# Filter phases by matmul with the turn's fraction left in PSUM, factors kept on chip, spatial weights transposed straight to their use

## The chip, the cores and the metric

One core of one Trainium2 chip. The metric is the device time of the whole kernel in microseconds (us), the median of several executions. PSUM is the memory that matmuls write, divided into banks; SBUF is the on-chip memory for everything else. Engines are named as in the profile: PE (matmuls), PEld (its weight loads), DVE (VectorE), ACT (ScalarE), POOL (GpSimd), SP (the sync engine, which issues most transfers).

## The reference, cut to what matters

```python
xn = layernorm(u)                                   # 2048 x 640, bf16
# A: a long convolution, filter K made from parameters
P  = exp(logdA[:, :, None] * l)                     # 640 x 128 x 2048, complex
K  = einsum('dn,dnl,dn->dl', Cc, P, dB).real        # 640 x 2048
yA = irfft(rfft(pad(xn.T)) * rfft(pad(K)))[:2048].T + xn * Dskip
# B: gated MLP with a product over positions
z  = gelu(xn @ w_in);  z1, z2 = z[:, :864], layernorm(z[:, 864:])
g  = w_sp @ z2 + b_sp[:, None]                      # w_sp 2048 x 2048
yB = (z1 * g) @ w_out
out = u + yA + yB
```

The kernel never forms P. It writes each power as a product of a coarse and a fine factor, each a magnitude (an exponential) times a sine or cosine, and contracts them by small matmuls in twenty chunks of 32 channels. Ten chunks make a half of the filter. Each half is expanded through DRAM, Fourier transformed, multiplied with the spectrum of u, and transformed back.

## The kernel before

All instructions of the kernel are ordered before the run: a list scheduler in the program estimates durations and picks, per engine, the ready instruction of the highest priority. So a priority or a wrong estimated duration changes the order that the chip later runs.

```python
op.prio = plen[op.gidx] + bmax + self.local.get(op.tag, 0.0)   # path length + bonus + bonus of its tag
...
MB_ = 100.0                                                    # bonus of the projections and the spatial product
...
B.local = dict(kcon=1000.0, kevac=1000.0)
```

A chunk: the phases are doubled up by ten integer adds on DVE, then two long sines and an absolute value on ACT, products on DVE, contraction on PE, and an eviction (PSUM to SBUF) in which four channels lie side by side.

```python
def phases(self, c):                        # cuts: copies
    for k in range(5):
        h = 1 << k
        B.tt("dve", F[:, h:2 * h, :], F[:, 0:h, :], ..., ALU.add)
    for k in range(5):
        ...                                 # the same for G
def trig(self, c):
    op = B.act(TR[:, n:2 * n], hi, ACTF.Sin, scale=SIN_SCALE, bias=SIN_BIAS)
    if c == 0:
        B.after(op, self.first_after)       # the first sine waits for the last GELU (one table swap)
    B.act(hi, hi, ACTF.Abs)
    B.act(TR[:, 0:n], hi, ACTF.Sin, scale=-SIN_SCALE, bias=math.pi / 2)
def contract(self, c):                      # cuts: 64 matmuls into pt
    B.tag = "kevac"
    B.flex(mk(K2, 4 * c % NB, [(NB, 2), (2 * NB, 65), (1, 4)]), mk(pt, 0, [(512, 2), (1, 65), (65, 4)]))
...
    for i in range(NPART):
        kg.chunks(max(NRES, 10 * i), 10 * i + 10)
        B.tt("dve", K2[:, 0:2 * NB], K2[:, 0:2 * NB], DSKM..., ALU.add)   # still tagged as before it
        cv.expand(i)                                                      # half i to DRAM and back
    for i in range(NPART):
        cv.forward_k(i, "k2", KP); cv.inverse1(i, "k2", KP)
```

The spatial weights w_sp are transposed to DRAM in the head and loaded from there; all factors of the filter are spilled to DRAM and loaded chunk by chunk.

Of the kernel before, what the change touches and what calls it, by code (L numbers as in the profile page):

```python
# [11 lines left out]
BF = DT.bfloat16  # L12
# [47 lines left out]
class Builder:  # L60
# [253 lines left out]

    def dma(self, out, in_, q="sp"):
        nb = self._dma_bytes(out)
        return self._add(q, lambda e: e.dma_start(out, in_), [in_], [out], is_dma=True, dur=0.45, lat=2.0 + nb / 250e3)  # L317

    def dma_transpose(self, out, in_, q="sp"):
        nb = self._dma_bytes(out)  # L320
        return self._add(q, lambda e: e.dma_start_transpose(out, in_), [in_], [out], is_dma=True, xbar=True, dur=1.5 if nb < 400000 else 2.6, lat=2.5)

    def schedule(self):
# [35 lines left out]
        cur_tab = None  # L359
        SEM = 0.08  # L360
# [4 lines left out]
        while nsched < n:  # L365
            bestq = None
            for q in QUEUES:
# [18 lines left out]
                for ts, op in evals:  # L386
                    if ts <= tmin + WIN:
                        if pick is None or op.prio > pick[1].prio:
                            pick = (ts, op)
                if bestq is None or pick[0] < bestq[0]:  # L390
                    bestq = (pick[0], pick[1], q)
# [5 lines left out]
            op.t1 = ts + op.dur + op.lat  # L397
# [172 lines left out]
class Arena:  # L570
# [7 lines left out]
    def want(self, name, nelem, dt, t0, t1, head=None):  # L578

        nb = (nelem * _dtsize(dt) + 63) // 64 * 64  # L580
        if head is None:
            pieces = [(0, nb, t0, t1)]
        else:
            h = head[0] * _dtsize(dt)
            pieces = [(0, h, t0, head[1]), (h, nb, t0, t1)]
# [86 lines left out]
NPW = 11  # L672
NE = 33
NT = 32
NRES = 5
NB = 40
NPART = 2
NF = 6
UB_ = 100.0
MB_ = 100.0  # L680
# [49 lines left out]
def _fft_consts():  # L730
# [12 lines left out]
    c2 = np.zeros((64, 32, 2, 2, 64))  # L743
    c2[:, :, 0, 0, :] = np.cos(th)
    c2[:, :, 1, 0, :] = np.sin(th)
    c2[:, :, 0, 1, :] = -np.sin(th)
    c2[:, :, 1, 1, :] = np.cos(th)
    c2 = c2.reshape(64, 32 * 256)
# [19 lines left out]

class Kgen:
# [3 lines left out]
    BONUS = 4.0  # L773

    def __init__(self, nc, B, ps, ar):
        self.B, self.ps, self.ar = B, ps, ar
        self.plb_d = nc.dram_tensor("plb_scratch", [128, NCH, (NGP + NFP) * CH], BF, kind="Internal")
        self.pli_d = nc.dram_tensor("pli_scratch", [128, NCH, (NPW + 1) * CH], I32, kind="Internal")
        self.wants()

    def wants(self):
        ar = self.ar
        ar.want("RAW", 6 * 5 * 128, BF, 0, 1)
        ar.want("LDT", D, BF, 0, 1)
        ar.want("DTB", D, BF, 1, 2)
        for n_ in ["al", "bt", "r1", "wre", "wim", "t3", "w2", "wab", "pp"]:
            ar.want("T" + n_, D, F32, 1, 2)
        ar.want("PW", D, I32, 1, 2)
        ar.want("PH2", D, I32, 1, 2)
        ar.want("DSKM", NPART * 2 * NB, BF, 0, 8)  # L790
        ar.want("PLB", NCH * (NGP + NFP) * CH, BF, 1.5, 2.4, head=(NRES * (NGP + NFP) * CH, 4.5))
        ar.want("PLI", NCH * (NPW + 1) * CH, I32, 1.5, 2.4, head=(NRES * (NPW + 1) * CH, 4.5))
        for i in range(2):
            ar.want("PH%d" % i, (NPW + NT + NE) * CH, I32, 2.6, 7)
            ar.want("PB%d" % i, (NGP + NFP) * CH, BF, 3.3, 7)
            ar.want("FT%d" % i, 2 * NT * CH, BF, 3.3, 7)
            ar.want("GT%d" % i, 2 * 65 * CH, BF, 3.3, 7)
            ar.want("TR%d" % i, (2 * (NT + NE) + NE) * CH, BF, 3.3, 7)
        ar.want("MG", 65 * CH, BF, 3.3, 7)
        ar.want("MF", NT * CH, BF, 3.3, 7)  # L800
        for i in range(NPART):
            ar.want("K2%d" % i, 65 * 2 * NB, BF, [4, 5][i], [7, 7.1][i])

    def pl(self, q):
        v = self.ar["PLB"].rearrange("p (c q x) -> p c q x", c=NCH, q=NGP + NFP)[:, :, q, :]
        return v.rearrange("p c (g j) -> p c g j", g=8)

    def ipl(self, q):
        v = self.ar["PLI"].rearrange("p (c q x) -> p c q x", c=NCH, q=NPW + 1)[:, :, q, :]
        return v.rearrange("p c (g j) -> p c g j", g=8)  # L810

    @staticmethod
    def cv(t):
        return t.rearrange("p (g c j) -> p c g j", g=8, c=NCH, j=4)

    def prep_loads(self, srcs, log_dt):
        B, ar = self.B, self.ar
        RAW = ar["RAW"].rearrange("p (a k n) -> p a k n", a=6, k=5)
        for a, src in enumerate(srcs):
            B.dma(RAW[:, a, :, :], src.rearrange("(k p) n -> p k n", p=128), q="act")  # L820
        B.dma(ar["LDT"], log_dt.partition_broadcast(128), q="act")

    def prep1(self, IDENT):
        B, ar = self.B, self.ar
        RAW = ar["RAW"].rearrange("p (a k n) -> p a k n", a=6, k=5)
        B.tag = "prep1"
        self.raw = {}
        for a, n_ in enumerate(["A", "Bt", "bre", "bim", "cre", "cim"]):
            pt = self.ps.bank("raw", [0, 1, 2, 3, 4, 5]).bitcast(BF)
            for k in range(5):  # L830
                B.transpose(pt[:, 128 * k:128 * k + 128], RAW[:, a, k, :], IDENT)
            self.raw[n_] = pt[:, 0:D]
        B.act(ar["DTB"], ar["LDT"], ACTF.Exp)

    def prep2(self):
        B, ar = self.B, self.ar
        T = {n_: ar["T" + n_] for n_ in ["al", "bt", "r1", "wre", "wim", "t3", "w2", "wab", "pp"]}
        R = self.raw
        DTB = ar["DTB"]
        B.tag = "prep2"  # L840
        al, bt, r1 = T["al"], T["bt"], T["r1"]
        B.tt("dve", al, R["A"], DTB, ALU.mult)
        B.stt(bt, R["Bt"], 1.0 / TWO_PI, DTB, ALU.mult, ALU.mult)
        alv = self.cv(al)
        B.memset("pool", self.pl(G_AG), 1.0)
        B.memset("pool", self.pl(G_BG), 1.0)
        B.memset("pool", self.pl(NGP + F_BF), 1.0)
        for k in range(1, 9):
            B.act(self.pl(G_AG + k), alv, ACTF.Exp, scale=float(8 * k))
        for j in range(1, 8):  # L850
            B.act(self.pl(G_BG + j), alv, ACTF.Exp, scale=float(j))
        for j in range(1, 8):
            B.act(self.pl(NGP + F_BF + j), alv, ACTF.Exp, scale=float(64 * j))
        for k in range(1, 4):
            B.act(self.pl(NGP + F_AWF + k), alv, ACTF.Exp, scale=float(512 * k))
        B.ts("dve", r1, bt, MAGIC, MAGIC, ALU.add, ALU.subtract)
        B.tt("dve", bt, bt, r1, ALU.subtract)
        B.ts("dve", self.ipl(0), self.cv(bt), 4294967296.0, None, ALU.mult)
        for k in range(1, NPW):
            B.ts("dve", self.ipl(k), self.ipl(0), k, None, ALU.logical_shift_left)  # L860
        wre, wim, t3, w2, wab, pp = T["wre"], T["wim"], T["t3"], T["w2"], T["wab"], T["pp"]
        bre, bim = r1, bt
        B.copy("act", w2, R["bre"])
        B.copy("act", pp, R["bim"])
        B.tt("dve", wre, R["cre"], w2, ALU.mult)
        B.tt("dve", t3, R["cim"], pp, ALU.mult)
        B.tt("dve", wre, wre, t3, ALU.subtract)
        B.tt("dve", wim, R["cre"], pp, ALU.mult)
        B.tt("dve", t3, R["cim"], w2, ALU.mult)
# [11 lines left out]
        B.tt("dve", self.ptmp_w(), wab, DTB, ALU.mult)  # L881
        wav = self.cv(self.ptmp_w())
        B.copy("dve", self.pl(NGP + F_AWF), wav)
        for k in range(1, 4):
            B.tt("dve", self.pl(NGP + F_AWF + k), self.pl(NGP + F_AWF + k), wav, ALU.mult)
        B.ts("dve", t3, wre, 0.0, -17179869184.0 / TWO_PI, ALU.is_lt, ALU.mult)
# [575 lines left out]
```

## Time and profile before

| | before |
|---|---|
| time | 598.35 us (597.88 to 602.45, 3 runs) |
| first sine (start of the chunks) | 202 us |
| chunks | 218 us, 10.9 each, DVE 84% busy |
| from the last contraction to the end | 178 us |
| bytes moved by DMA | 85.49 MB |
| mean granted PE clock | 0.81 |

The page's slices show that no engine is full throughout, so the time is a sum of stages, and each must be read with its own table; the prediction below quotes those lines. Lines of a timeline: start, duration, what; "ACTq" is the issue of a transfer by ScalarE's queue.

```profile
L237 ACT ACTIVATE arena<-arena 128x640 bf16<-128x640 f32 x25 | 15.8, 720 | 0.0
```

```profile
11.56 1.09 ACTq L317 DMA_DIRECT2D arena<-c_c  x1
12.68 1.28 ACT L236 ACT_TABLE_LOAD   x1 [12.68 <-issue]
```

Twenty-five exponentials take 15.8 us; ScalarE is free of issuing transfers at 12.7 us and starts the normalisation.

### The profile page before, as it was taken

What the parts mean: (1) busy time and instruction counts of PE and PEld (TensorE: products, weight loads), DVE (VectorE), ACT (ScalarE), POOL (GpSimd) and SP (SyncE); (2) the same over time, 40 slices, a digit from 0 to 9 for tenths busy, and PEclk for the clock granted to TensorE, in tenths of its full rate; (3) what the DMA queues carried; (4) which work ended last, traced back from release to release, by engine and by line L of the source; (5) the groups of instructions that cost most, each with busy time, mean ns of one, the idle gap of its engine ahead of it and who ended that gap; (6) DMA issues with size and microseconds to landing.
All of it is one profiled execution on the core that took longest, in us unless ns stands there. A gap on an engine that the chain in (4) does not pass through costs nothing.

```text
span 598.8 us, 9933 instructions
## 1 busy us (share of the span) xinstructions
PE 359.5 (60%) x4096; PEld 225.9 (38%) x4118; DVE 341.4 (57%) x664; ACT 283.1 (47%) x262; POOL 11.2 (2%) x19
## 2 busy tenths in 40 slices
PE   0064036379999876148887898832016366668774
PEld 0052014134544443134443445412004255567663
DVE  4399024259942197898997889985004443732221
ACT  1978613133554858655864854844005325622000
POOL 1200000000000000000000000000000000000000
PEclk9977555779999988669998989975557569669998
DMA  9999999996273510015124112117548854774212
GB/s 275 224 262 305 223 232 337 339 291 174 67 268 102 167 42 14 4 40 198 30 84 146 30 31 60 29 48 223 48 73 265 187 100 137 249 159 88 59 46 54
DMA packets 119196, 85.49 MB, mean 143 GB/s; under 512 B 91532, under 2 KB 109808, under 8 KB 117872
## 3 DMA queue, kind: packets, MB, share of 16 engines
q1 hardware_dynamic: 114928, 81.62, 50.5%
q10 hardware_dynamic: 4224, 3.24, 1.9%
q8 instruction: 32, 0.52, 0.4%
q14 instruction: 12, 0.10, 0.0%
HBM read 45.78 MB, written 30.67 MB: 128 GB/s over the span
## 4 chain that ended last, share of the span: by engine, by line
PE 22%; DVE 20%; ACT 12%; SPq 8%; DMA 5%; issue 4%; DVEq 0%; ACTq 0%
PE ps L304 22%; DVE arena L247 19%; ACT arena L237 11%; SPq L317 8%; DMA arena<-uh_scratch 4%; DMA k2d_scratch<-arena 1%; DVE arena L254 0%; ACT L237 0%; DVE arena L278 0%; DVE arena L267 0%; DVEq L555 0%; DVEq L532 0%; SPq L535 0%; DVEq L535 0%; ACTq L532 0%
## 5 line engine op out<-in xcount | busy, mean ns | idle before, releaser
L304 PE MATMUL ps<-arena 128*32 128x65 bf16 (+9 forms) x3986 | 348.1, 295 | 196.7 <-DVE arena L247 90.0
L304 PEld LDWEIGHTS ps<-arena 128*128 128x128 bf16 (+6 forms) x4008 | 215.5, 120 | 328.8 <-issue 131.0
L237 ACT ACTIVATE arena<-ps 128x1024 bf16<-128x1024 f32 (+7 forms) x126 | 111.4, 917 | 244.1 <-PE ps L304 208.0
L247 DVE TENSOR_TENSOR arena<-arena 128x2048 bf16<-128x2048 bf16 (+7 forms) x164 | 142.1, 913 | 49.5 <-ACT arena L237 32.3
L237 ACT ACTIVATE arena<-arena 128x2080 bf16<-128x2080 int16 (+4 forms) x95 | 147.7, 1617 | 3.7 <-DVE arena L267 2.5
L278 DVE CAST arena<-ps 128x1024 bf16<-128x1024 f32 (+3 forms) x38 | 44.6, 1176 | 121.8 <-PE ps L304 101.3
L247 DVE CUSTOM_DVE_ANT_0 arena<-arena 128x128 uint16<-128x128 uint16 (+5 forms) x202 | 59.3, 362 | 3.5 <-DMA pli_scratch<-arena 3.4
L247 DVE TENSOR_TENSOR arena<-ps,arena 128x512 bf16<-128x512 f32 (+3 forms) x49 | 34.8, 742 | 44.5 <-PE ps L304 44.3
L254 DVE TENSOR_SCALAR arena<-arena 128x1056 bf16<-128x1056 bf16 (+7 forms) x75 | 28.1, 412 | 16.8 <-ACT arena L236 10.3
L307 PE MATMUL ps<-arena 128*128 128x128 bf16 x110 | 11.8, 294 | 35.0 <-DMA arena<-c_ident 30.7
L1253 DVE BATCH_NORM_STATS2 arena<-arena 128x6 f32<-128x432 bf16 (+1 forms) x48 | 24.0, 558 | 9.8 <-DMA arena<-in_A_u_dram 6.1
L307 PEld LDWEIGHTS ps<-arena 128*128 128x128 bf16 x110 | 10.5, 136 | 36.3 <-issue 31.1
L236 ACT ACTIVATE arena<-arena 128x640 bf16<-128x640 bf16 x16 | 11.8, 736 | 0.5
L245 POOL TENSOR_TENSOR arena<-arena 128x4 f32<-128x4 f32 x8 | 8.7, 1094 | 86.8 <-DVE arena L254 85.8
L237 ACT ACT_TABLE_LOAD x8 | 10.3, 1283 | 0.1
L267 DVE COPY arena<-arena 128x32 int32<-128x32 int32 (+1 forms) x45 | 7.4, 169 | 2.5 <-DMA pli_scratch<-arena 2.5
L236 ACT ACT_TABLE_LOAD x1 | 1.3, 1283 | 12.7 <-issue 12.7
L878 DVE RECIPROCAL arena<-arena 128x640 f32<-128x640 f32 x1 | 4.2, 4153 | 0.0
L259 DVE SCALAR_TENSOR_TENSOR arena<-arena 128x4 f32<-128x4 f32 (+2 forms) x13 | 2.5, 204 | 2.1 <-POOL arena L245 1.9
L271 POOL MEMSET arena<- 128x640 bf16 (+3 forms) x7 | 2.2, 355 | 67.8 <-DMA pli_scratch<-arena 67.5
L278 DVE COPY arena<-ps 128x1024 bf16<-128x1024 bf16 x2 | 2.4, 1224 | 1.2 <-PE ps L307 1.2
L236 ACT ACTIVATION_READ_ACCUMULATOR arena<-arena 128x1 f32 x16 | 3.0, 186 | 0.0
(7 smaller groups left out, 5.0 us busy)
## 6 DMA issues: line engine op xcount, KB each, us to landing
arena<-uh_scratch SPq DMA_DIRECT2D x20, 480.0 KB, 5.1
wt_scratch<-arena SPq DMA_DIRECT2D x16, 512.0 KB, 4.7
arena<-wt_scratch SPq DMA_DIRECT2D x4, 2048.0 KB, 8.3
arena<-in_A_u_dram SPq DMA_DIRECT2D x8, 640.0 KB, 8.2
uh_scratch<-arena SPq DMA_DIRECT2D x10, 480.0 KB, 3.1
plb_scratch<-arena SPq DMA_DIRECT2D x3, 1160.0 KB, 10.6
arena<-plb_scratch SPq DMA_DIRECT2D x15, 232.0 KB, 2.6
pli_scratch<-arena SPq DMA_DIRECT2D x3, 960.0 KB, 5.1
```

The source lines that it names most:

```text
L236: return e.activation(out, in_, func, bias=bias, scale=scale, accum_out=accum_out)
L237: return e.activation(out, in_, func, bias=bias, scale=scale)
L245: return self._add(q, lambda e: e.tensor_tensor(out, in0, in1, op), [in0, in1], [out], dur=d, port=True)
L247: return self._add(q, lambda e: e.tensor_tensor(out, in0, in1, op), [in0, in1], [out], dur=self._dve_cost("tt", out, [in0, in1]), port=port)
L254: return self._add(q, lambda e: e.tensor_scalar(out, in0, s1, s2, op0, op1), self._aps(in0, s1, s2), [out], dur=self._dve_cost("ts", out, ...
L267: return self._add(q, lambda e: e.tensor_copy(out, in_), [in_], [out], dur=self._dve_cost("ts", out, [in_]), port=not self._is_psum(in_))
L278: "dve": (lambda e: e.tensor_copy(out, in_), self._dve_cost("ts", out, [in_]))}
L304: return self._add("pe", lambda e: e.matmul(out, lhsT, rhs, start=start, stop=stop, **kw), [lhsT, rhs], [out], dur=d)
L307: return self._add("pe", lambda e: e.transpose(out, in_, ident), [in_, ident], [out], dur=0.06)
L317: return self._add(q, lambda e: e.dma_start(out, in_), [in_], [out], is_dma=True, dur=0.45, lat=2.0 + nb / 250e3)
L878: B.generic("dve", lambda e: e.reciprocal(t3, pp), [pp], [t3], dur=4.2)
L1253: B.generic("dve", (lambda e, c=c: e.bn_stats(st[:, a, c, :], src[:, a, w * c:w * c + w])), [src[:, a, w * c:w * c + w]], [st[:, a, c, :]] ...
```

## The change

The intent: phases come from matmuls (constants times phase parts, with 192 added so that the low 16 bits of the fp32 result are the fraction of a turn), so that DVE loses its adds and ACT the absolute value; the factors stay on chip; w_sp is transposed in 64 pieces straight into the buffers of its use; each half of the filter is expanded as soon as it is ready, in 37 transfers; the spectrum's buffers are halved.

```diff
-MB_ = 100.0
+NF = 3                       # was 6: rows of the spectrum per load and product
+MB_ = 0.0
+CPP = 10
@@ phases and sines: the ten adds of a chunk go
+        def sin(dst, lhsT, rhs):
+            bank = self.ps.bank("ph", [6, 7])
+            B.mm(bank, lhsT, rhs)
+            op = B.act(dst, bank.bitcast(I16)[:, 0:1024:2], ACTF.Sin, scale=SIN_SCALE)
+            if c == 0:
+                for o in self.first_after: B.after(op, o)      # all GELUs
@@ factors: the order of channels is now (chunk, group) with the chunk innermost
-        return t.rearrange("p (g c j) -> p c g j", g=8, c=NCH, j=4)
+        return mk(t, 80 * i, [(1, CPP), (160, 4), (CPP, NJ)])
+        for i in range(2):
+            alv = self.cv(ar["TAL"], i)
+            for k in range(1, 9):
+                B.act(self.pl(i, G_AG + k), alv, ACTF.Exp, scale=float(8 * k))
@@ eviction of a chunk
-        B.flex(mk(K2, 4 * c % NB, [(NB, 2), (2 * NB, 65), (1, 4)]), mk(pt, 0, [(512, 2), (1, 65), (65, 4)]))
+        B.flex(mk(K2, c % CPP, [(65 * NB, 2), (NB, 65), (CPP, 4)]), mk(pt, 0, [(512, 2), (1, 65), (65, 4)]))
@@ spatial weights
-        B.dma(ar["WS%d" % (c % 2)]..., wt_d...[:, :, 512 * c:512 * c + 512])
+            for b in range(8):
+                op = B.dma_transpose(w[:, b, :], B_w_sp[512 * c:512 * c + 512, ...])
+                B.after(op, cv.last_u)
@@ order of the program
-    for i in range(NPART): kg.chunks(...); ...; cv.expand(i)
+    kg.chunks(0, CPP); dskip_expand(0); [spatial product]
+    kg.chunks(CPP, 2 * CPP); cv.first_k("k2", KP); dskip_expand(1)
+    cv.forward_k(0, ...); cv.inverse1(0, ...); cv.first_k(...); cv.forward_k(1, ...); cv.inverse1(1, ...)
-    B.local = dict(kcon=1000.0, kevac=1000.0)
+    B.local = dict(kcon=1000.0, kevac=1000.0, kpe=500.0, load=2000.0, wload=-200.0)
```

Cut: the scheduler's transfer model, the splitting of phases into bf16 parts, the Fourier constants, buffer lifetimes.

## The prediction

> **What bounds the kernel now.** I read the page first (shares and the 40 slices), then a table of busy times by stage, then the groups by shape, then the chain of waits, and last the sync engine's timeline where the chain named it.
>
> ```profile
> PE 359.5 (60%) x4096; PEld 225.9 (38%) x4118; DVE 341.4 (57%) x664; ACT 283.1 (47%) x262; POOL 11.2 (2%) x19
> ...
> PE   0064036379999876148887898832016366668774
> ...
> DVE  4399024259942197898997889985004443732221
> ACT  1978613133554858655864854844005325622000
> ...
> PEclk9977555779999988669998989975557569669998
> DMA  9999999996273510015124112117548854774212
> ```
>
> No engine is full over the span, and the full one changes: DMA in the first nine slices, PE in slices 10 to 13, DVE in the middle, nobody in slices 28 to 30. So there are stages. The table by stage (length; then busy us of PE, weight load, DVE, ACT, POOL; granted clock; DMA share; GB/s):
>
> ```profile
> 0.00:45.00 45.00, 9.92 (x94) 8.69 (x94) 24.97 (x69) 28.59 (x50) 6.31 (x13) 0.93 0.99 254
> 45.00:203.00 158.00, 99.51 (x653) 52.29 (x661) 75.75 (x147) 71.98 (x85) 4.84 (x6) 0.78 0.78 223
> 203.00:421.00 218.00, 152.00 (x1734) 81.10 (x1747) 183.40 (x370) 137.81 (x82) 0.00 (x0) 0.86 0.26 78
> 421.00:545.00 124.00, 61.95 (x717) 51.54 (x718) 44.49 (x63) 44.67 (x47) 0.00 (x0) 0.67 0.65 154
> 545.00:599.00 54.00, 36.16 (x904) 32.30 (x900) 12.73 (x16) 0.00 (x0) 0.00 (x0) 0.96 0.20 51
> ```
>
> Head (0 to 203): normalisation, input projections, spectrum of u. The DMA engines are saturated to about 140 us, PE has only 109 us of work. Filter stage (203 to 421): twenty chunks; DVE is busy 84% and sets the pace at 218/20 = 10.9 us a chunk. Tail (421 to 545): filter spectrum, product, first inverse; PE half idle. End (545 to 599): output projection. What a chunk costs is in the groups by shape:
>
> ```profile
> L237 ACT ACTIVATE arena<-arena 128x2080 bf16<-128x2080 int16 x40 | 76.2, 1928 | 2.9 <-DVE arena L267 2.5
> L237 ACT ACTIVATE arena<-arena 128x2080 int16<-128x2080 int16 x20 | 50.3, 2521 | 0.3
> L247 DVE CUSTOM_DVE_ANT_0 arena<-arena 128x1024 uint16<-128x1024 uint16 x40 | 25.9, 683 | 0.0
> L247 DVE CUSTOM_DVE_ANT_0 arena<-arena 128x512 uint16<-128x512 uint16 x40 | 15.0, 417 | 0.0
> L237 ACT ACTIVATE arena<-ps 128x520 bf16<-128x520 f32 x19 | 11.5, 603 | 76.6 <-PE ps L304 70.3 <-DVE arena L247 6.3
> ```
>
> The first two are the two sines and the absolute value of each chunk, the next two the larger of ten 32-bit integer adds that double up the phases. The last is the yardstick for a ScalarE read of about 512 PSUM columns. The chain of waits alternates DVE and ACT through this stage, then becomes the sync engine; its timeline and the list of waits say why:
>
> ```profile
> 402.50 3.41 SPq L317 DMA_DIRECT2D k2d_scratch<-arena  x4
> ...
> 411.07 34.39 SPq L317 DMA_DIRECT2D arena<-k2d_scratch  x50
> ```
>
> ```profile
> PE ps L304 <- DMA arena<-xn_scratch: 28.7, 1, 28.7
> PE ps L304 <- DMA arena<-k2d_scratch: 27.4, 1, 27.4
> ```
>
> Fifty small expansions of half 0 of the filter are issued only at 411, though its chunks were done much earlier, and PE waits 27 us. The 28.7 us is the head's equivalent: PE waits for the reordered u, whose transfers share the DMA engines with the round trip of the spatial weights.
>
> **What the Trainium skill says.** ScalarE: Activation LUTs, "What ACT_TABLE_LOAD costs", gives 186 ns + 0.833 ns per element for an ACTIVATE with immediate scale and bias, with about 93 ns overlapped back to back. The trace agrees: 619 predicted against 603 for 520 columns, 1919 against 1928 for 2080. TensorE: Matmul & The Clock Gate, "What's actually happening", says an idle PE falls to half clock and recovers after some us of activity; the slices agree (0.5 where PE is idle, 0.9 and more in the dense slices 9 to 13). DMA: Bandwidth & Descriptors, "Specifications", asks for 512 B or more per transfer for line rate; the tail agrees, at DMA share 0.65 only 154 GB/s move, against 254 GB/s at 0.99 in the head. "Issuing engines are not separate DMA queues" on the same page says that all queues share the 16 DMA engines, which is why the weight round trip can delay u.
>
> **The change part by part.**
>
> Phases. Per chunk DVE loses the ten adds, 2 x (683+417+283+221+184) = 3.6 us by mean durations, 2.86 us as the timeline shows a run of ten, plus one or two copies at 0.17. It gains only one instruction, because the negated-sine product is split in two. From the timeline the rest is 1.13+0.16+0.62 for magnitudes and 0.42+3.5 for products: about 5.9 us a chunk against 9.0. The gate adds 28 x 0.68 = 19 us per kernel, 0.95 a chunk in both. ACT now has eight sines of 512 from PSUM: 0.603 less the overlap, 0.52 each, 4.2 us, against 12.5 us for two chunks in the timeline, 6.25 each; the absolute value is gone since the cosine gets its quarter turn in the matmul. PE gains eight matmuls of 512 columns per chunk. The spatial matmuls ran 30 in 6.68 us, 0.223 each, so 1.8 us a chunk, 36 us in all. So a chunk wants DVE 6.9, ACT 4.8 with its eviction, PE 1.8 + 2.0 for the contraction, plus the spatial matmuls as filler. With two of eight banks for phases and the stalls seen before (10.9 measured against 9.95 summed), I say 8.0 us a chunk: 160 instead of 218, minus 58.
>
> Head. Gone: spatial weights transposed to DRAM and back (16.8 MB written and read, by the issue list) and the spill of factors, 3 x (1160+960) KB written and as much read, 12.7 MB. New: phase parts written and read, some 3 MB in pieces of 256 B and 2.5 KB. The 64 smaller transposes wait behind the last load of u. In the first 140 us some 39 MB moved at 280 GB/s; without about 23 of them the same loads need some 60 us. Identity and w_in come first, so PE, which idled to 30.7 and then from 55 to 83, can start at 40 and go on. Its head work is about 100 us (99.5 busy, part at low clock). Spectrum of u shares banks with the phases, so the first sine waits for all of it: u lands near 62, then 42 evictions of about 1.0 to 1.2 us with their matmuls take some 60 to 70 us. First sine at about 130 instead of 201.7, minus 72.
>
> Tail. Expansion of half 0 moves under the chunks; half 1 has 8 writes and 29 reads instead of 50, at 0.62 us of issue each some 23 us, plus two landings of 3 to 8 us: about 37. Half 0's spectrum, product and inverse took 447 to 498 with a wait of 14 inside, so they cover it. What is left: half 0 about 42 less a first stage done earlier, half 1 47 (498 to 545), end 54: 143, plus some 5 because loads now come in half-size groups: 148 instead of 599 - 421 = 178, minus 30.
>
> By the chain: 130 + 160 + 148 = 438. But PE becomes a second bound. Its busy time 359.5 + 36, less about 15 for a higher clock, is 380. It is idle 40 at the start, and the end stays 54 for 36 busy. The other 344 at the best density seen, 45.1 of 50 us between 150 and 200 (0.90), need 382: 40 + 382 + 54 = 476. Two bounds so close disturb each other, so I take the larger and a little more: **482 us**.
>
> **The rivals.** (1) PE takes the place of DVE completely: phases, contraction and spatial matmuls all sit in the chunk stage, 36 + 40 + 106 = 182 us for a stage of 160, and the in-order queue delays phases behind spatial matmuls waiting for weights. For it: the order is fixed before the run from estimated durations. Against it: spatial matmuls have lowest priority and can move into the tail, where PE is half idle. Time: 520 to 545. (2) The weight transposes become the new wait: three buffers of half a block, and each new half block needs 8 transposes; before, a transpose held the sync queue a median 3.3 us (up to 16). At 3.3 for each of 64 that is 211 us of issue, and they stand in one queue with the expansions. For it: only three buffers. Against it: a quarter of the bytes each, and the old median was taken under saturated DMA. Time: 530 to 560. (3) The head's transfers were hidden anyway: the projections and the spectrum of u take PE and evictions to about 180 in any case. Against it: PE idles 28.7 us on u alone. Time: about 525. (4) Everything fits and PE stays dense: 440.
>
> **Range and chances.** The rivals that cost most stop near 560, still 6% under 598; a loss needs two of them and a third that I don't see, such as the tables of GELU and sine being swapped many times. The range is 440 (chain alone) to 535 (one rival in full). Faster by over 2%: 0.95; within 2%: 0.03; slower: 0.02.
>
> **What would show it.** Integer adds gone from the DVE groups and 160 sines of 128x512 from PSUM near 0.6 us; if they take 1 us, ScalarE is the bound. First sine at 110 to 155. Last contraction near 300, chunks about 8 us apart. From there to the end about 150, with no wait of PE on the expansion over 10 us. PE busy 370 to 400 with a granted clock over 0.85, against 0.81. DMA about 57 MB instead of 85.5. Wrong would be: DMA still at 0.9 and more beyond 100 us, PE waiting tens of us for the spatial weights, or a sine stage paced by PE's queue.

## The result, and the profile after

The changed kernel takes **629.13 us** (623.75 to 630.64, 4 runs) against 598.12 for the kernel before in the same rounds. Ratios here and below are the mean time of one kernel's fast runs over that of the other's fast runs of the same rounds, so not quite the ratio of the medians: 1.0493, with a 95% interval of 1.0423 to 1.0563. It is slower, and the prediction, 482, is wrong by far.

The page after, busy times and three of its slices:

```profile
PE 444.8 (71%) x4264; PEld 236.1 (38%) x4264; DVE 302.8 (48%) x506; ACT 294.5 (47%) x382; POOL 11.7 (2%) x24
...
PE   0046502895698978777666766894689999997996
...
ACT  0686798353534776867877676510013541100000
...
PEclk9999755997679998776666556697799999996998
```

Before, PE was half idle in the stage after the chunks; now it is full there (slices 31 to 36), while in the chunks (slices 15 to 25) neither PE nor ACT is full and PE's clock sinks to 0.6 and 0.5. The table by stage (length, then busy us of PE, PEld, DVE, ACT, POOL; clock, DMA share, GB/s):

```profile
0.00:52.00 52.00, 11.23 (x89) 7.85 (x90) 24.71 (x69) 26.38 (x49) 7.14 (x16) 1.00 0.65 218
52.00:106.00 54.00, 14.66 (x69) 6.74 (x66) 31.27 (x51) 46.62 (x64) 1.01 (x1) 0.68 0.46 97
106.00:214.00 108.00, 87.91 (x589) 46.26 (x590) 44.04 (x75) 46.58 (x51) 3.52 (x7) 0.84 0.39 103
214.00:397.00 183.00, 131.08 (x1512) 55.56 (x1511) 118.97 (x161) 135.22 (x183) 0.00 (x0) 0.68 0.13 24
397.00:571.00 174.00, 147.82 (x1172) 81.03 (x1171) 71.61 (x137) 39.66 (x39) 0.00 (x0) 0.92 0.66 149
```

| | before | predicted | after |
|---|---|---|---|
| first sine | 202 | 130 | 214 |
| chunks | 218 (10.9 each) | 160 (8.0) | 183 (9.1) |
| last contraction to end | 178 | 148 | 232 |
| DMA, MB | 85.5 | 57 | 60.8 |
| PE busy / clock | 360 / 0.81 | 370 to 400 / over 0.85 | 445 / 0.82 |

The predicted chain of 438 us is missed by 84 + 23 + 84 = 191 us, which is 438 to 629. All three stages contribute. What was to go has gone: the DMA share in the head is 0.65, 0.46 and 0.39 instead of 0.99 and 0.78, the integer adds are absent, and PE's wait for the expansion is no longer in the list of waits. Other things came. In the groups of instructions (busy us, mean ns, idle time ahead of them):

```profile
L237 ACT ACTIVATE arena<-ps 128x512 bf16<-128x512 int16 x160 | 94.2, 632 | 11.7 <-PE ps L304 11.4
L304 PE MATMUL ps<-arena 98*128 98x512 bf16 x160 | 77.4, 532 | 48.2 <-ACT arena L237 47.3
...
L237 ACT ACTIVATE arena<-ps 128x520 bf16<-128x520 f32 x20 | 49.8, 2492 | 33.6 <-PE ps L304 33.6
...
L237 ACT ACTIVATE arena<-arena 128x320 bf16<-128x320 f32 x50 | 32.8, 756 | 0.0
```

The sines are near the prediction: 0.59 us busy each (94.2/160), where it named 0.6 as the sign and put 0.52 into its sum. But the eviction of a chunk takes 2492 ns where the same 520 columns took 603 before, and half as long exponentials (320 instead of 640) take longer each (756 against 720 ns), so 32.8 us for the same number of elements that took 15.8. The phase matmuls last 532 ns, and PE waited 47 us ahead of them for ACT. The chain of waits through the chunk stage (224 to 397 us) is PE for 52% and ACT for 47%, in turn: with two PSUM banks for the phases the two engines release each other, so what ACT loses is lost to the chunk, though no engine is full.

ScalarE's timeline shows the exponentials as one block in the head, and PE's shows who waits for it:

```profile
71.62 32.78 ACT L237 ACTIVATE arena<-arena 128x320 bf16<-128x320 f32 x50
```

```profile
106.65 3.78 PE L304 MATMUL ps<-arena 128*128 128x432 bf16 x10 [32.10 <-ACT arena L237]
```

PE stands 32 us until the GELU behind the block has freed its PSUM bank. Earlier still, ScalarE's queue is issuing loads:

```profile
6.15 6.77 ACTq L332 DMA_DIRECT2D arena<-in_A_A_im_dram  x1
12.95 5.49 ACTq L332 DMA_DIRECT2D arena<-in_A_A_re_dram  x1
18.46 2.69 ACTq L332 DMA_DIRECT2D arena<-in_A_log_dt_dram  x2
21.19 1.28 ACT L236 ACT_TABLE_LOAD   x1 [21.19 <-issue]
```

The normalisation begins at 21.2 instead of 12.7 us. The kernel before issues the same loads from the same queue (A_im took 0.46 us there and A_re 2.90); why they take longer now was not tried. Last, the sync engine's timeline of the tail:

```profile
318.35 22.60 SPq L332 DMA_DIRECT2D arena<-k2d_scratch  x29
...
411.80 6.13 SPq L336 DMA_TRANSPOSE arena<-in_B_w_sp_dram  x4
```

The expansion of half 0 did move under the chunks (318 instead of 411 us), as intended. But the transposes that feed the second spatial block start only at 412, after the chunks. Of 476 spatial matmuls about 72 run in the chunk stage (1512 instructions less 160 for phases and 1280 for the contraction), which is one filling of the four PSUM banks (4 x 17 = 68). The gate that empties a bank, a DVE product, first runs at 389.7 us.

### The profile page after: what moved, and what is told of

It reads as the page before. It is cut to its first block, busy times and chain, and to the rows that moved or that the text cites. A ratio compares the mean times of both kernels' runs of the same rounds, so it can differ in the third digit from the quotient of the medians.

```text
span 628.8 us, 10204 instructions
## 1 busy us (share of the span) xinstructions
PE 444.8 (71%) x4264; PEld 236.1 (38%) x4264; DVE 302.8 (48%) x506; ACT 294.5 (47%) x382; POOL 11.7 (2%) x24
## 4 chain that ended last, share of the span: by engine, by line
PE 45%; ACT 27%; DMA 8%; DVE 6%; SPq 5%; issue 3%; ACTq 3%; POOL 1%; DVEq 0%
PE ps L304 45%; ACT arena L237 25%; DMA arena<-uh_scratch 4%; SPq L332 4%; ACTq L332 3%; DVE arena L247 2%; DMA arena<-in_A_u_dram 2%; DVE arena L278 2%; DMA uh_scratch<-arena 2%; SPq L336 2%; ACT arena L236 1%; ACT L237 1%; DVE arena L1308 1%; DVE arena L925 1%; DVE arena L254 1%
## 5 line engine op out<-in xcount | busy, mean ns | idle before, releaser
L304 PE MATMUL ps<-arena 128*32 128x65 bf16 (+9 forms) x4178 | 434.0, 300 | 137.6 <-ACT arena L237 114.0
L304 PEld LDWEIGHTS ps<-arena 128*128 128x128 bf16 (+5 forms) x4178 | 228.6, 118 | 342.8 <-ACT arena L237 195.4
L237 ACT ACTIVATE arena<-ps 128x512 bf16<-128x512 int16 (+8 forms) x282 | 230.8, 888 | 237.5 <-PE ps L304 164.6
L247 DVE TENSOR_TENSOR arena<-arena 128x480 bf16<-128x480 bf16 (+8 forms) x230 | 156.5, 721 | 120.8 <-ACT arena L237 78.0
L278 DVE CAST arena<-ps 128x1024 bf16<-128x1024 f32 (+1 forms) x40 | 48.0, 1200 | 74.7 <-PE ps L304 67.0
L237 ACT ACTIVATE arena<-arena 128x320 bf16<-128x320 f32 (+2 forms) x60 | 40.5, 764 | 1.2 <-DVE arena L247 0.9
L307 PE MATMUL ps<-arena 128*128 128x128 bf16 (+1 forms) x86 | 10.9, 296 | 40.8 <-DVE arena L254 35.6
L254 DVE TENSOR_SCALAR arena<-arena 128x1056 bf16<-128x1056 bf16 (+5 forms) x65 | 24.3, 401 | 20.5 <-ACT arena L236 19.5
L307 PEld LDWEIGHTS ps<-arena 128*128 128x128 bf16 (+1 forms) x86 | 7.5, 131 | 44.0 <-DVE arena L254 36.8
L236 ACT ACT_TABLE_LOAD x1 | 1.3, 1283 | 21.2 <-issue 21.2
L259 DVE SCALAR_TENSOR_TENSOR arena<-arena 128x4 f32<-128x4 f32 (+3 forms) x17 | 6.0, 356 | 4.3 <-POOL arena L245 4.1
```

What stands on the lines that cost most here:

```text
L236: return e.activation(out, in_, func, bias=bias, scale=scale, accum_out=accum_out)
L237: return e.activation(out, in_, func, bias=bias, scale=scale)
L247: return self._add(q, lambda e: e.tensor_tensor(out, in0, in1, op), [in0, in1], [out], dur=self._dve_cost("tt", out, [in0, in1]), port=port)
L254: return self._add(q, lambda e: e.tensor_scalar(out, in0, s1, s2, op0, op1), self._aps(in0, s1, s2), [out], dur=self._dve_cost("ts", out, ...
L278: "dve": (lambda e: e.tensor_copy(out, in_), self._dve_cost("ts", out, [in_]))}
L304: return self._add("pe", lambda e: e.matmul(out, lhsT, rhs, start=start, stop=stop, **kw), [lhsT, rhs], [out], dur=d)
```

## The experiments

Four theories at the start. **Eviction**: the chunk pace is set by the strided eviction. **Gates**: the spatial product stands since its gates lose to the chunks' work on DVE (path length, bonus 100 to 0), so 100 us of PE work fall behind the chunks. **Exponentials**: their layout holds the head. **Rival to all**: PE has too much work, or its order and its two PSUM banks for the phases set the pace, whatever ACT does. Fifteen kernels ran, in four batches, each timed in three rounds beside the kernel before. The comparison with the reference passed in all but the one named. Each batch ran on another chip, so runs of different batches are compared by their ratios to the kernel before. Medians of the kernel before: 600.9 in the first batch (a1 to a4), 599.75 (b1 to b4), 598.27 (d1 to d4), 598.55 (e1 to e3).

**a1_gate: gates first.**

```diff
-    B.local = dict(kcon=1000.0, kevac=1000.0, kpe=500.0, load=2000.0, wload=-200.0)
+    B.local = dict(kcon=1000.0, kevac=1000.0, kpe=500.0, load=2000.0, wload=-200.0, gate=500.0)
```

> The changed kernel with one constant added: the gate multiplications on VectorE get a scheduling priority of 500, so that they are placed among the filter chunks. Theory S (starved gate: with priority zero the gates were all put behind the chunks, so the spatial matmuls filled their four PSUM banks once and then stood still until the chunks were done): the spatial matmuls move into the chunk stage, the stretch between the last chunk and the output projection shrinks from about 170 to about 110 us, the granted clock in the chunk stage rises from 0.53-0.73 to over 0.85, and the time falls from 629 to 570-595. Theory P (PE simply has too much work after the change): the chunks slow down by what the tail gains, time within 2% of 629.

Measured 620.15 us, ratio 1.0326 (1.0245 to 1.0406), 10 us better than the change by the ratios (0.0167 x 598). Spatial matmuls do move in (1629 PE instructions in the chunk stage instead of 1512), but the chunks, 9.6 us apart, are slower, and the clock of the stage is 0.79, not over 0.85. So theory S missed its 570 to 595; the chunk stage grew by 10 us and the rest shrank by 14, about as theory P had it. The gates are a cause, of small size here.

**a2_evac_dve: the eviction on VectorE.**

```diff
-        B.flex(mk(K2, c % CPP, [(65 * NB, 2), (NB, 65), (CPP, 4)]), ...)
+        B.copy("dve", mk(K2, c % CPP, [(65 * NB, 2), (NB, 65), (CPP, 4)]), ...)
```

> The changed kernel with the evacuation of each chunk's filter rows (128x520 from PSUM, written to every tenth bf16) on VectorE instead of ScalarE. Theory E (the 2.49 us that this takes on ScalarE, against 0.60 before, paces the chunks, because sines and evacuation stand in one queue): chunks go from 9.1 us apart to 7.0-7.5, the time falls by 30 to 40 us, to 590-600. If the strided write is as slow on VectorE (over 2 us), the chunks become VectorE-bound at about 8.5 us and the gain is under 12 us. Theory P/S: chunk pace is not set by the evacuation, gain under 10 us.

Measured 618.19 us, ratio 1.0276 (1.0215 to 1.0338), chunks 8.7 us apart. Its group:

```profile
L267 DVE CAST arena<-ps 128x520 bf16<-128x520 f32 x20 | 49.4, 2472 | 6.2 <-PE ps L304 6.2
```

The other engine needs about as long, 2.47 us. So the cost belongs to the access and not to ScalarE, and the outcome is the one written for a write that is slow on VectorE too (8.5 us a chunk), with 13 us gained instead of under 12.

**a3_both: both of these.**

> Both edits of the two runs before together. If starved gates and slow evacuation are separate costs, the gains add: 545-565. If they hide behind each other (the chunk stage becomes PE-bound once the spatial matmuls are in it), the time is no better than the better of the two less 10 us.

Measured 594.79 us, ratio 0.9881 (0.9799 to 0.9963). Taken off ScalarE, and with the gates let through, the two together gain 37 us (0.0612 x 598), more than 10 and 13, though short of the 545 to 565 that were expected. PE has 1737 instructions in the chunk stage, more than a1's, so with ACT relieved there seems to be room in the stage for what the gates let in.

**a4_evac_runs: the same eviction in runs of four.** The result is wrong, since the channels land in another order than their readers assume. The comparison with the reference passed all the same, so its tolerance doesn't notice these channels changing places.

```diff
-        B.flex(mk(K2, c % CPP, [(65 * NB, 2), (NB, 65), (CPP, 4)]), ...)
+        B.flex(mk(K2, 4 * (c % CPP), [(65 * NB, 2), (NB, 65), (1, 4)]), ...)
```

> The changed kernel with the evacuation left on ScalarE but written in runs of four neighbouring bf16 (8 bytes), as before the change did; the channels then land in the wrong order, so the result is wrong on purpose. Theory E1 (it is the stride of the 2-byte writes that costs): 128x520 evacuation at about 0.60 us instead of 2.49, chunks at 7.0-7.5 us, time 590-600. Rival E2 (reading PSUM while matmuls write the neighbouring banks makes it slow): it stays near 2.5 us and the time near 629.

Measured 585.42 us, ratio 0.9724 (0.9652 to 0.9796), chunks 7.0 us apart instead of 9.1. Its group:

```profile
L237 ACT ACTIVATE arena<-ps 128x520 bf16<-128x520 f32 x20 | 12.1, 605 | 33.8 <-PE ps L304 33.8
```

Same engine, same 520 elements, 605 ns instead of 2492. The eviction theory stands. The rival E2 falls, and of the rival to all this much, that two banks allow 7.0. What sets the 7.0 is another matter: in b1, below, the chain through the chunks is still PE (52%) and ACT (43%) in turn.

**b1_fix, b2_fix_gate, b3_fix_gate_exp: mended for good.** The readers of the filter now take the permuted column (first Fourier stage of u, inverse, skip term), so the result is right; that rests on following the indices, as the comparison can't tell. b2 adds the gates' priority, b3 stores the exponentials' fp32 source in the order in which they read it.

```diff
+        B.flex(mk(K2, 4 * (c % CPP), [(65 * NB, 2), (NB, 65), (1, 4)]), ...)
+                col = q + k if T == NB else CPP * k + q // 4           # first stage, u only
+                    pcol = 4 * ((b0 + k) % CPP) + (b0 + k) // CPP       # inverse
+        K2 = mk(ar["K2%d" % i], 0, [(65 * NB, 2), (4, CPP), (1, 4)])    # skip term
@@ b2: gate=500.0
@@ b3
-        B.tt("dve", ar["TAL"], pa[:, 0:D], DTB, ALU.mult)
+        for i in range(2):
+            v = [mk(t, 80 * i, [(160, 4), (CPP, NJ), (1, CPP)]) for t in (pa, DTB)]
+            B.tt("dve", mk(ar["TAL"], 320 * i, [(NJ, 4), (1, NJ), (4 * NJ, CPP)]), v[0], v[1], ALU.mult)
-            alv = self.cv(ar["TAL"], i)
+            alv = mk(ar["TAL"], 320 * i, [(4 * NJ, CPP), (NJ, 4), (1, NJ)])
```

> The run with runs of four bf16, made correct: the order of channels inside a half is carried through by reading columns in another order in the first stage of u's spectrum, in the first inverse and in the skip term; no instruction is added. Theory E1 (the stride of the 2-byte writes): as the wrong-result run, 580-590, correct. If the permuted reads cost something on PE or VectorE: over 595.

> The corrected kernel plus priority 500 for the gates. The gate priority alone gave 9 us of 629, and 23 us when the evacuation had been moved to VectorE. Theory S (starved gates; the gain was hidden because the chunk stage was paced by the evacuation): another 20 to 35 us off the corrected kernel, 552-567. Theory P (PE's order and amount of work is the bound): under 10 us.

> As the run before, and the 50 exponentials read a row that VectorE wrote in their own order, instead of fp32 elements 40 bytes apart. Theory X (the scattered read doubles each of them, 0.66 us instead of 0.36, and the first projections wait behind them): the block of 50 takes 18 instead of 33 us, the first sine comes 10 to 15 us earlier than 213, time 540-555. Rival (the head is set by u's reordering or by PE): first sine within 3 us, time unchanged.

Measured: b1 586.11 us, ratio 0.9788 (0.9735 to 0.9841); b2 571.16, 0.9553 (0.9494 to 0.9613); b3 555.9, 0.9291 (0.9248 to 0.9335). As differences of ratios times 598: the eviction is worth 42 us, the gates 14, the exponentials 16. The gates gave less than the 20 to 35 expected, the exponentials a little more in the head (first sine 18 us earlier, not 10 to 15). In b3:

```profile
L304 PE MATMUL ps<-arena 98*128 98x512 bf16 x160 | 59.0, 388 | 10.0 <-ACT arena L237 8.1
L237 ACT ACTIVATE arena<-arena 128x320 bf16<-128x320 f32 x50 | 18.2, 453 | 0.0
```

and its chunk stage (columns as in the tables by stage):

```profile
195.00:338.00 143.00, 131.36 (x1628) 61.40 (x1627) 122.64 (x166) 99.82 (x183) 0.00 (x0) 1.00 0.24 45
```

The exponentials fall from 756 to 453 ns. PE, which waited 47 us for ACT at its phase matmuls, waits 8, and the matmuls themselves fall from 532 to 388 ns, as the stage's clock rose from 0.68 to 1.00.

**b4_before_expand: the kernel before, with half 0 expanded early.** One line gives the skip term the priority of the evictions.

```diff
+        B.tag = "kevac"
         B.tt("dve", K2[:, 0:2 * NB], K2[:, 0:2 * NB], ar["DSKM"]..., ALU.add)
```

> The kernel before with one line: the addition of the skip term is tagged so that it gets the priority of the chunk's evacuation, so the expansion of half 0 can start after its tenth chunk. This is the part of the change that frees the tail, alone. Prediction's tail theory: PE's wait of 27 us for the expansion goes, the time falls by 15 to 27 us to 571-584. Rival (the transfers only move to where they delay something else): under 6 us.

Measured 567.6 us, ratio 0.9474 (0.9413 to 0.9534), a little better than expected. PE's wait for the expansion fell from 27.4 to 1.9 us:

```profile
PE ps L304 <- DMA arena<-k2d_scratch: 1.9, 1, 1.9
```

From the last contraction to the end it is 148 us, 31 us less than in the kernel before. That is the tail that the prediction had for the change, so all that it hoped for there is had from the old kernel by one word.

**d1_exp_alone: the change with its exponentials in order, nothing else.** (The edit of b3 alone.)

> The changed kernel with one thing mended: the exponentials read their fp32 source in order instead of 40 B apart; the strided eviction and the starved gates stay. Theory (ScalarE's 33 us of exponentials hold the whole head, so what they lose moves the first sine): exponentials 756 to about 453 ns, first sine from 214 to about 196, and nothing after it changes, so the time falls by about 15 to 18 us: 611 to 616, about 1.02 to 1.025 of the kernel before. Rival (the head is set by late loads of u and by PE's order; the gain in the other build came from the gates): first sine at 210 or later, time 622 to 630.

Measured 611.69 us, ratio 1.0208 (1.0175 to 1.024): 17 us, the same as on top of the other two remedies. The first sine moved from 213.9 to 198.3. The head's share of this cause is settled.

**d2_banks: b3 with four PSUM banks for the phases.**

```diff
-    PH = [6, 7]
+    PH = [2, 3, 6, 7]
-            pt = ps.bank("m", [0, 1, 2, 3])[0:M, :]
+            pt = ps.bank("m", [0, 1])[0:M, :]
```

> The three remedies (eviction in runs of four, gates first, exponentials in order), 555.9 before, plus four PSUM banks for the phases instead of two, the spatial matmuls' banks cut from four to two. Theory (at 6.6 us a chunk ScalarE waits for PE between sines, because only two banks alternate): sines back to back, 8 x 0.53 + 0.6 of eviction = 4.8, DVE then sets the pace at about 6.0 us; 20 chunks gain some 10 us: 545 to 550. Rival (the pace is already DVE's, and two banks leave the spatial matmuls nothing to overlap with the gate): chunks stay at 6.5 or more and the time is 556 to 570.

Measured 551.97 us, ratio 0.9218 (0.9186 to 0.9249), 4 us better than b3 by the ratios (their intervals just touch), so between the two expectations, and not in the way of the theory:

```profile
L237 ACT ACTIVATE arena<-ps 128x512 bf16<-128x512 int16 x160 | 82.2, 612 | 57.7 <-DVE arena L247 52.7 <-PE ps L304 5.0
```

ScalarE's sines no longer wait for PE but 53 us for DVE, and the evictions are 7.6 us apart, slower than b3's 7.0. The chain of waits changes: in b3's chunks it is PE (51%) and ACT (46%) in turn and hardly DVE (1%), here PE (67%) and DVE (18%). So two banks did tie PE and ACT together, as the theory had it, but loosening them made no chunk faster: over the 154 us from the first sine to the last contraction PE is busy 148 and DVE 138, and DVE took over 17 of the 20 evictions, since the scheduler may choose their engine. What moved with the small gain is PE's work: 148 us in the stage against 131 in b3, so less was left behind it (200 us to the end instead of 216).

**d3_prio: b3 with the spatial product's bonus of 100 given back.**

```diff
-MB_ = 0.0
+MB_ = 100.0
```

> The three remedies plus the old bonus of 100 for the spatial matmuls (0 in the change). Theory (spatial matmuls left behind the chunks cost PE time in the tail one for one, so more of them under the chunks is a gain): their last gate moves from about 490 to before 430, chunks slow from 6.6 to about 7.5, tail falls from 223 by 35 or more, time 540 to 552. Rival (the tail is set by the chain of expansion, spectrum, product, inverse, in whose gaps the spatial matmuls lie for nothing; moving them up only slows the chunks): time 560 to 580.

Measured 580.35 us, ratio 0.9692 (0.9664 to 0.9719), 24 us worse than b3. The chunks keep their pace (6.9 us). The table by stage tells where it went (the first line is the chunks):

```profile
193.00:336.00 143.00, 130.37 (x1603) 60.48 (x1620) 123.01 (x167) 96.72 (x181) 0.00 (x0) 0.99 0.29 58
336.00:405.00 69.00, 66.15 (x299) 29.78 (x303) 14.68 (x22) 3.56 (x5) 0.00 (x0) 1.00 0.52 132
405.00:520.00 115.00, 58.94 (x658) 47.02 (x659) 50.47 (x106) 38.84 (x40) 0.00 (x0) 0.66 0.54 120
```

Behind the chunks PE does the rest of the spatial product for 69 us, nearly full, and then the spectra for 115 us, half idle at a clock of 0.66. In b3 the two lie over each other. So in the tail the spatial matmuls are a filler for a chain with gaps, and in the mended kernel the bonus of 0 is right.

**d4_head: b3, with the small loads issued by the sync engine.**

```diff
-            B.dma(RAW[:, k, :, :], srcs[a]..., q="act")
+            B.dma(RAW[:, k, :, :], srcs[a]...)            # and the two of log_dt
```

> The three remedies, plus the eight small parameter loads issued by the sync engine behind x instead of by ScalarE, whose queue is held by them until 20.5 us, so that its first work of the normalisation starts at 21 (about 13 in the kernel before). Theory (that delay is carried to the first sine): ScalarE's first activation at about 12, first sine from 195 to about 187, time 546 to 550. Rival (the head waits for the loads of u and PE's order, not for the normalisation): first sine within 3 us of 195, time 553 to 558.

Measured 541.19 us, ratio 0.9029 (0.8993 to 0.9065), more than expected. ScalarE's timeline:

```profile
5.28 0.74 ACT L236 ACTIVATE arena<-arena 128x640 bf16<-128x640 bf16 x1 [3.27 <-DMA arena<-in_A_u_dram]
```

Its first activation is at 5.3 instead of 22.6 us, the first sine at 180.7 instead of 195.4. The 16 us by the ratio are carried in full to the end. The rival, that the head waits for u and PE's order, falls for this part. The edit does two things at once: it frees ScalarE, and the parameters, queued behind x, are in SBUF sooner (A_re at 14.4 instead of 27.0 us in the change). The first activation shows the first; what the second gave was not tried apart.

**e3_mm2_eighth: d4 with 2 of the 16 blocks of the spatial product.** Wrong (relative error 0.042).

```diff
-        for h in range(2):                 # 16 transposes a block of rows
+        for h in range(1):
-            for b in range(8):
+            for b in range(2):
-            for b in range(16):
+            for b in range(2):
```

> The build with the early normalisation (541.2 before), with the spatial product cut to 2 of its 16 blocks and their transposes (result wrong on purpose): 392 of 448 long matmuls, some 85 us of PE work, and 56 of 64 weight transposes gone. Theory A (the tail, 216 us here from the last contraction to the end where 148 were predicted, is long because spatial matmuls and their weights lie in it): the tail falls to about 150 and the time to 470 to 480. Theory B (the tail is a chain of expansion, U loads, product and inverse of two half filters, in whose gaps the spatial work lies nearly for nothing): the tail falls by less than 30, time 512 to 535.

Measured 529.06 us, ratio 0.885 (0.8817 to 0.8883). Most of the spatial work gone saves 11 us by the ratios (0.0179 x 598). The table by stage (d4 first, then this kernel; chunks, spectra and inverse, end):

```profile
181.00:324.00 143.00, 129.72 (x1605) 61.07 (x1624) 122.64 (x166) 99.76 (x184) 0.00 (x0) 1.00 0.24 45
324.00:480.00 156.00, 120.68 (x951) 68.60 (x965) 68.19 (x130) 37.14 (x38) 0.00 (x0) 0.89 0.62 148
480.00:540.00 60.00, 52.82 (x933) 38.93 (x930) 13.11 (x16) 0.00 (x0) 0.00 (x0) 0.94 0.21 58
```

```profile
181.00:341.00 160.00, 130.86 (x1525) 56.19 (x1527) 134.30 (x185) 99.70 (x183) 0.00 (x0) 0.74 0.24 46
341.00:468.00 127.00, 62.67 (x676) 49.17 (x674) 55.23 (x110) 37.83 (x39) 0.00 (x0) 0.64 0.50 137
468.00:527.00 59.00, 51.07 (x931) 37.12 (x928) 13.11 (x16) 0.00 (x0) 0.00 (x0) 0.95 0.21 58
```

From the last contraction to the end it is 186 us without the spatial work and 216 with it: 30 us of the tail belong to it, at the edge of what was written for theory B, and 186 are a chain of their own, where 148 were predicted. The chunk stage grew by 17 us; not its pace, which is 7.0 in both, but its start: the shrunk spatial product sends its 28 gates to DVE at once, and the second eviction comes 22 us after the first. So the spatial matmuls don't set the chunk pace. The chain through the chunks is PE (53%) and ACT (42%) in turn here too, now at a clock of 0.68.

**e2_uh_act: d4, with the loads of the spectrum of u issued by ScalarE.**

```diff
-                      self.uh_d[64 * s:64 * s + 128, i, :, ...])
+                      self.uh_d[64 * s:64 * s + 128, i, :, ...], q="act")
```

> The build with the early normalisation (541.2), with one thing moved: the loads of U for the product, 44 small ones that stand in the sync engine's queue among 29 expansions and the weight transposes, are issued by ScalarE. Theory (the queue's order holds them: VectorE's product of half 0 waits 46 us for them): those waits fall below 25 us, the product of half 0 ends by 385 instead of 400, time 525 to 533. Rival (the loads wait for their two buffers and for bandwidth, not for the queue; and ScalarE's evictions now wait behind them): waits stay near 45 us and the time is 538 to 550.

Measured 536.22 us, ratio 0.8979 (0.8934 to 0.9024), between the two expectations; its interval overlaps that of d4, so a gain is not shown. The list of waits, d4 and this kernel:

```profile
DVE arena L247 <- DMA arena<-uh_scratch: 46.0, 18, 13.3
```

```profile
DVE arena L247 <- DMA arena<-uh_scratch: 13.4, 11, 2.4
```

The waits vanish nearly as hoped, and the product of half 0 ends at 392 instead of 399 us: the order of one issuing queue did hold the loads, but the chain has other links behind them (evictions, one buffer for both halves) that take most of it back.

**e1_banks_head: d4 and d2 together.**

> The two gains found apart put together: early normalisation (541.2) and four PSUM banks for the phases (which took 555.9 to 552.0). If they are independent, 541.2 - 3.9 = 537; if the second bank pair only helped through the tail's order, 541 to 545.

Measured 536.87 us, ratio 0.8984 (0.8949 to 0.9019). The 537 that was expected if the two gains are independent, though the interval overlaps that of d4 by a little, so the second gain is not clear of noise. With e2, level with it, this is the best correct version: 10% below the kernel before and 15% below the change (536.87 / 629.13 = 0.853).

## Why the prediction was wrong, point by point

**Phases.** DVE's sum was right: adds gone, DVE busy 303 instead of 341, and in the chunk stage, where hardly a gate runs, 119.0/20 = 5.9 us a chunk, the 5.9 that it had without the gate. ScalarE's term "4.8 with its eviction" failed: the eviction was put at the old 0.603 us and took 2.49, since the change writes it 20 bytes apart. The form of the sum failed with it: it asked each engine for its work and took the largest, DVE's 6.9, with an allowance for stalls, while the chain runs through PE and ACT in turn, so that the 1.9 us more of each eviction were paid in full. A chunk takes 9.1 us instead of 8.0, and instead of the 7.0 that the same kernel reaches with runs of four (a4, b1), which is better than predicted. Worth 42 us in all (b1). PE's term "0.223 each, 36 us" was too small as well: the phase matmuls are busy for 77.4 us, and still for 59.0 with the clock at 1.00 (b3).

**"The spatial matmuls as filler"** failed next: their gates lost on DVE to the chunks, and one filling of four banks was all that ran there. The sign named in the prediction, a clock over 0.85, failed to come: 0.82 in the whole and 0.68 in the stage, with phase matmuls of 532 instead of 388 ns. But sized on the chip this is only 10 (a1) to 14 us (b2), because in the tail the same matmuls lie in the gaps of a chain (d3, e3). Rival (2) of the prediction, that the weight transposes become the new wait, did not come: a transpose takes a median 1.26 us of issue instead of 3.3, and PE waits 9.7 us for weights in all, not tens. The transposes do come late, but since their buffers come free late: their queue waits 72 us for PE.

**Head: first sine at 214 instead of 130.** "Loads need some 60 us, so PE can start at 40 and go on" failed. The bytes did vanish, and PE's wait of 28.7 us for the reordered u with them, but the first sine came no earlier: the transfers were not what PE would wait for next. Three pieces make the 84 us. The exponentials, read 40 bytes apart, held PE for 32 us (16 us of the first sine, d1). ScalarE's queue was held by issuing loads until 21 us (15 us, d4). The other 53 us have no run of their own: with both mended the first sine is at 181 in d4. PE's work up to the first sine is 114 us in the change (11.2 + 14.7 + 87.9 by stage) where the prediction counted about 100, and the first sine waits for the last of it by an explicit dependency on all GELUs, where the prediction counted only the spectrum of u. Nor did PE "go on": from 40 to 181 us in d4 it is busy 96 of 141. How the order of projection, spectrum and second projection makes these gaps was not tried and stays open. Rival (3), "hidden anyway", came nearest, with 180 us for this work; that d4 has 181 may be luck.

**Tail: 232 instead of 148.** The wait on the expansion (27 us) was removed as predicted, and in the old kernel that alone makes a tail of 148 us (b4). The term that failed is "half 0 about 42 less a first stage done earlier": in e3, with hardly any spatial work, half 0 takes from 341 to about 402 and half 1 to 468, 127 us for both, where the prediction had 42 + 47 = 89 and b4 needs about 94 (148 less the 54 of the end). Why they take longer is argued and not shown: the halves now share single buffers, and the U loads come as 40 of 240 KB at a median 3.4 us instead of 20 of 480 KB at 5.1, in one queue with expansions and transposes. On the chain of waits the landing of U loads holds 24% of e3's 127 us against 10% of b4's 94, but e2, which took DVE's wait for them from 46 to 13 us, gained little. The end takes 58 us instead of 54. Spatial work makes another 30 of the 216. The change itself has 232; letting the gates through shortened the tail from 232 (b1) to 217 (b2), so they are the rest. What e2 left of the chain was not taken further.

**Sum.** "Two bounds so close, so I take the larger" decided nothing, since the chain alone was 191 us short. PE's busy time of 445 instead of 380 came only in part from its low clock: in d4, at 0.91, it is 414, with 59 for the phases instead of 36 and, in the end, 53 instead of 36. The chances, 0.95 for faster, rested on rivals that each move work between engines; none asked what a change of layout does to instructions that keep their name and count. The range, to 535, also left out the upper ends of its own rivals (1) and (2), 545 and 560. By the ratios, the four causes explain 629 to 541: eviction 42, gates 14, exponentials 16, issuing 16. What d4 still lacks against the predicted chain of 438 is the rest of the head (51 us) and of the tail (69), less 18 that its chunks are faster than predicted.

Three small slips of the prediction cost nothing. 85.5 MB less 16.8 and 12.7 and plus 3 is 59 MB, not 57; 60.8 moved. And 154 GB/s at a share of 0.65 and 254 at 0.99 are 237 and 257 per full share, so they hardly show that short transfers are slow; the packets of the tail do, with 95 GB/s per full share under 512 B and 335 from 2 KB up. The clock of 0.5 "where PE is idle" leaves out the first two slices, where PE is idle and the clock reads 0.9.

That the layouts can matter could have been looked up. The Trainium skill, Advanced Engine Details and Errata, "SBUF Cachelines", says that accesses that go to a different 16-byte line each pay a penalty, and strides of 20 and 40 bytes do so. The runs agree: 2492 against 605 ns, 756 against 453. That the lines are the reason was not tested apart from the stride.

## What to carry to other kernels

When a change touches the order of data, go through every instruction that keeps its count and ask in which steps it now reads and writes: an eviction that runs only twenty times, four times as long, cost 42 us in a change that had removed two hundred adds. Where two engines release each other in turn, add their times along the chain; the largest of the engines' sums is only a lower bound (here DVE's 6.9 us against a chain of PE and ACT of 9.1). Removing a bound pays only up to the next one, so read which chain stands right behind it; here, ScalarE's queue issuing loads stood behind the transfers, and PE's own work behind that. Where a static order is made from estimated durations, a wrong estimate or priority is itself a cost, and one priority is a cheap experiment to run first, on the old kernel too.

## What the Trainium skill lacked or had wrong

- ScalarE: Activation LUTs, "What ACT_TABLE_LOAD costs", gives one cost per element and says nothing of the access pattern. It held for 603 and 605 ns (runs of four bf16), but not for 520 bf16 written 20 bytes apart: 2492 ns, 4.8 ns an element. Nor for fp32 read 40 bytes apart: 756 ns for 320 elements against 453 in order.
- Advanced Engine Details and Errata, "SBUF Cachelines", names the penalty but no size. For these patterns it is a factor of 4.1 on the write and 1.7 on the read.
- Vector Engine (DVE) Microarchitecture Reference, "5.2 Measured stream behaviour on trn2", has 2.5 ns per column for a destination stepping 24 words. The 2-byte case measured here, 520 elements at 20 bytes on VectorE from PSUM, is 2472 ns, 4.75 ns an element, and is not in its table.
- DMA: Bandwidth & Descriptors, "Issuing engines are not separate DMA queues", says that issuing from several engines saves only the time on the sequencer, "which is usually small relative to the DMA itself". At the start of this kernel it was not small: two loads held ScalarE for 6.77 and 5.49 us, and landed 20.6 and 14.1 us after the start of their issue. Giving eight small loads to the sync engine was worth 16 us of the whole time (d4).
